# Last query group of an agent-attention and maxout kernel: four of six feature blocks multiplied as pairs of 64-row products in two PSUM banks

## The chip, the cores and the metric

The kernel runs on one core of one Trainium2 chip. The metric is device time in microseconds, the median of several runs. The engines have short names below: PE is TensorE (matrix products; PEld its weight loads), DVE is VectorE, ACT is ScalarE, POOL is GpSimd, and SP is SyncE, which issues the transfers.

## What is computed

Four batches of 12544 query rows with 128 channels attend to 49 agent rows, and the agents attend to all keys. The result goes through a feed-forward layer of width 768 with three input matrices and a maximum over them:

```python
a2k = softmax(agents @ k.T * scale)          # 49 x 12544 a batch
agent_v = a2k @ v                            # 49 x 128
q2a = softmax(q @ agents.T * scale)          # 12544 x 49
x = q2a @ agent_v
h = np.maximum(np.maximum(x @ w1, x @ w2), x @ w3)
out = h @ w_out                              # 50176 x 128, float32
```

## The kernel before

**Tiling.** A batch has 98 tiles of 128 query rows. The kernel works on groups of eight tiles (1024 rows). Groups 0 to 47 hold eight tiles of one batch each; group 48, the last, holds the two tiles that are left of each of the four batches. The agents' values are multiplied into the weights beforehand (tiles G, one a batch), so that a group goes straight from its exponentials to the hidden features. The 768 features are six blocks of 128, numbered f = 0 to 5. The eight tiles of a group are kept as four pairs jj = 0 to 3: the first tile of a pair lies in the upper 64 rows (49 of them used) of the exponentials e.s, the second in the lower 64.

**The operations of a group s**, with the names that the order list uses:
- `u.s.f` and `v.s.f` (PE, `hidden`, L558): the differences w3 - w1 (or w3 - w2 for f = 4) and w2 - w1, for all eight tiles. Each product has 49 rows; products for the upper rows (h = 0) and the lower rows (h = 1) alternate and write different banks. In group 48 each batch has its own G, so that a `u` or `v` is eight products of 128 columns there.
- `a.s.f` (ACT, L571, or L565 for f = 4) takes the positive part of u; `x.s.f` (DVE, L574) takes the maximum with v and writes r.s.f, tile R. For f = 4 v is added onto a in PSUM and ACT writes r.s.4 (L568). r.s.f holds all eight tiles of one feature block, as [128 features, h, 512].
- `li.s.o` (PE, `out_linear`, L582): the part of the output that is linear in x, for half o of the group (pairs 2o and 2o + 1), as two products of 128 rows and 256 columns. It opens the output bank o.s.o.
- `p.s.o.f` (PE, `out_hidden`, L592): four products of 128 rows (the features) and 128 columns that add block f to the half o.
- `su.s`, `re.s`: sums of the exponentials and their reciprocals.
- `ov.s.o` (DVE, `out_scale`, L599): the half o times the reciprocals, into rows 4o to 4o + 3 of the output tile OS.
- `st.s` (SP, L607): the store; in group 48 it is four transfers, each of two rows of OS (one batch).

**What sets the order.** `graph` lists the operations with their costs and needs, but the sequence that runs is the hand-stored list `ORDER` at the end of the file. It is one list for all engines; each engine works off its own operations in that order, and waits are put in where a tile's maker or last reader is on another engine. A number behind a slash names the buffer: `li.48.1/1` opens bank 1 of the class OM, which has two. Bank 1 was that of `o.47.1` and is free when `ov.47.1` has read it; bank 0 was that of `o.47.0`. The `cost` and `mode` given to `add` are notes for a planner and change nothing in the program.

The end of the list before:

```
a.48.4 u.48.3/1 p.47.1.5 x.48.5/11 p.47.1.1 li.48.0/0 a.48.3/0 p.48.0.1 p.48.0.0 v.48.4 ov.47.1 v.48.3/0 x.48.4/7 p.48.0.2
x.48.3/0 st.47 p.48.0.5 li.48.1/1 p.48.1.2 p.48.1.5 p.48.1.4 p.48.0.4 p.48.0.3 p.48.1.3 ov.48.0/2 p.48.1.1 p.48.1.0 ov.48.1 st.48
```

Of the kernel before, what the change touches and what calls it, by code (L numbers as in the profile page):

```python
# [12 lines left out]
ALU = mybir.AluOpType  # L13

P, H, C, A, B, NT, GT, KT, NF = 128, 64, 128, 49, 4, 98, 8, 9, 6
# [4 lines left out]
C31, C21, C1O, WC = 0, DFF, 2 * DFF, 2 * DFF + 2 * C  # L20
CV, CS, CT = KT * A, KT * A + A, (KT - 1) * A
FI = 4
SPARE = 8
FIRST = [KT] * 10 + [4, 4]
LATER = [KT] * 10 + [8]
# [2 lines left out]
PE, ACT, DVE, POOL, SP = range(5)  # L28
ROW, FULL, COL = range(3)
# [11 lines left out]
class Plan:  # L41
# [5 lines left out]
    def add(self, name, eng, fn, cost, mode=FULL, after=(), new=(), use=(), bank=None, serve=0.0):  # L47
        self.index[name] = len(self.ops)
        for cls, t in new:
            self.tiles[t] = cls  # L50
            self.maker[t] = name
        seq = [self.maker[t] for t in use if self.maker[t] not in after]
        self.ops.append(dict(name=name, eng=eng, fn=fn, pace=cost[0], lat=cost[1], mode=mode, after=list(after), seq=seq,
                             new=[t for _, t in new], use=[t for _, t in new] + list(use), bank=bank, serve=serve))
# [21 lines left out]
def parts_of(s):  # L76

    if s < B * WHOLE:
        return [(s // WHOLE, s % WHOLE * GT, GT, 0, GT // 2)]
    return [(b, WHOLE * GT, 2, b, 1) for b in range(B)]  # L80
# [14 lines left out]
def mm(n, cols):  # L95
    t = n * max(cols / 2400 + 0.0025, 0.0253)
    return t, t + 0.235
# [18 lines left out]
def graph(plan, em):  # L116
    add = plan.add
# [4 lines left out]
    for g, (t0, n) in enumerate(ch):  # L122
# [3 lines left out]
            new=[("KB", f"kb0.{g}")], use=[f"k0.{g}"])  # L126
# [4 lines left out]
            new=[("EK", f"e0.{g}")], use=[f"s0.{g}"])  # L131
        add(f"to0.{g}", PE, em.totals(g, n), mm(1, n * 49), after=[f"kx0.{g}"], new=[("OM", "acc")] if g == 0 else [],
            use=[f"e0.{g}"] + (["acc"] if g else []))
        m = n if n == KT else 2
        add(f"vc0.{g}", ACT, em.cast("v", "vb", 0, t0, n, ACT, 0, m), act(m * 128), after=[f"vl0.{g}"], new=[("VB", f"vb0.{g}")],
            use=[f"v0.{g}"])
        if m < n:
            add(f"vd0.{g}", DVE, em.cast("v", "vb", 0, t0, n, DVE, m, n), ((n - m) * 0.067 + 0.08, (n - m) * 0.067 + 0.2),
                after=[f"vl0.{g}"], use=[f"v0.{g}", f"vb0.{g}"])
        add(f"kv0.{g}", PE, em.first_values(g, n), mm(n, 49), after=[f"to0.{g}", f"vc0.{g}"] + ([f"vd0.{g}"] if m < n else []),  # L140
            use=[f"vb0.{g}", f"e0.{g}", "acc"])
# [3 lines left out]
    for w in ("w1", "w3", "w2"):  # L145
# [3 lines left out]
    add("d31a", DVE, em.differences(C31, "w3", "w1", ((0, DFF // 2),)), (0.43, 0.55), after=["lw1a", "lw3a"], use=["w1", "w3"])  # L149
    add("d31b", DVE, em.differences(C31, "w3", "w1", ((DFF // 2, FI * P), (FI * P + P, DFF))), (0.42, 0.54), after=["lw1b", "lw3b"],  # L150
        use=["w1", "w3"])
# [9 lines left out]
        use=["kr0", "acc"])  # L161
    half = DFF // 2
    for name, c, d, eng in (("a", C31, ["d31a"], ACT), ("b", C31 + half, ["d31b", "d32"], DVE), ("c", C21, ["d21a"], ACT),
# [3 lines left out]
            after=[f"gp{name}"], use=[f"gp{name}", "G0"])  # L167
# [7 lines left out]
    for b in range(1, B):  # L175
        ch = chunks(b)
        for g, (t0, n) in enumerate(ch):
            r, m = f"{b}.{g}", f"m.{host_of(b, g)}"
# [10 lines left out]
                use=[m], bank=m)  # L189
            add(f"kv{r}", PE, em.values(b, g, n, m), mm(n, 49), after=[f"kx{r}", f"vc{r}"], use=[m, f"vb{r}", f"e{r}"], bank=m)  # L190
            add(f"va{r}", DVE, em.add_values(b, g, m), (0.13, 0.25), after=[f"kv{r}"] + ([f"va{b}.{g - 1}"] if g else []),
                new=[] if g else [("VA", f"va{b}")], use=[m] + ([f"va{b}"] if g else []), bank=m)
            if g < len(ch) - 1:
                add(f"ea{r}", POOL, em.add_exps(b, g), (0.97, 1.06), after=[f"kx{r}"] + ([f"ea{b}.{g - 1}"] if g else []),
                    new=[] if g else [("EA", f"ea{b}")], use=[f"e{r}"] + ([f"ea{b}"] if g else []))
# [3 lines left out]
            use=[m, f"es{b}", f"e{r}"], bank=m)  # L199
        add(f"nr{b}", DVE, em.normalise(b, m), (0.5, 0.62), after=[f"to{b}", f"va{r}"], new=[("KR", f"kr{b}"), ("G", f"G{b}")],  # L200
            use=[m, f"va{b}"], bank=m)
        for name, c0, c1, eng in (("a", C31, C31 + DFF, ACT), ("c", C21, C21 + DFF, DVE), ("l", C1O, WC, ACT)):
            w = c1 - c0
            add(f"gp{name}{b}", PE, em.product(b, c0, c1, f"gp{name}{b}"), mm(1, w), mode=COL, after=[f"nr{b}", "el"],
                new=[("UV" if w > 512 else "OM", f"gp{name}{b}")])
            add(f"gv{name}{b}", eng, em.product_out(b, c0, c1, c0, f"gp{name}{b}", eng), act(w) if eng == ACT else dve(w),
                after=[f"gp{name}{b}"], use=[f"gp{name}{b}", f"G{b}"])


    for s in range(NQ):  # L210
        parts = parts_of(s)
        gs = [f"G{p[0]}" for p in parts]
        add(f"ql.{s}", SP, em.q_load(s), new=[("LD", f"q.{s}")], **dma(524))
        add(f"qc.{s}", POOL, em.q_cast(s), (1.0, 1.1), after=[f"ql.{s}"], new=[("QB", f"qb.{s}")], use=[f"q.{s}"])
        if s in TURNED:
            add(f"qd.{s}", SP, em.turn_by_dma("qb.", "qT.", s, GT), (1.3, 1.0), after=[f"qc.{s}"], new=[("QT", f"qT.{s}")], use=[f"qb.{s}"],
                serve=0.255 * GT)
        else:
            add(f"qt.{s}", PE, em.q_turn(s), mm(GT, 128), after=[f"qc.{s}", "prep"], new=[("OM", f"qT_ps.{s}")], use=[f"qb.{s}"])
            add(f"qe.{s}", DVE, em.q_evacuate(s), (0.636, 0.735), after=[f"qt.{s}"], new=[("QT", f"qT.{s}")], use=[f"qT_ps.{s}"])  # L220
        add(f"sc.{s}", PE, em.q_scores(s), mm(len(parts), 512 // len(parts)), mode=COL, after=[f"qd.{s}" if s in TURNED else f"qe.{s}"],
            new=[("OM", f"qs.{s}")], use=[f"qT.{s}"])
        add(f"ex.{s}", ACT, em.q_exps(s), (0.56, 0.65), after=[f"sc.{s}"], new=[("EQ", f"e.{s}")], use=[f"qs.{s}"])
        m = f"m.{s}"
        h = s in hosting
        add(f"su.{s}", PE, em.sums(s, m, not h), mm(GT // 2, 2), after=[f"ex.{s}"] + ([f"ks{b}.{g}" for b in range(1, B)
            for g in range(len(LATER)) if host_of(b, g) == s] if h else []), new=[] if h else [("OM", m)], use=[f"e.{s}"] + ([m] if h else []),
            bank=m)
        add(f"re.{s}", DVE, em.recips(s, m), (0.13, 0.25), after=[f"su.{s}"], new=[("RC", f"rc.{s}")], use=[m], bank=m)
        for f in range(NF):  # L230
            def needs(base, first, second):
                out = []
                for p in parts:
                    out.append(f"gv{first if f < 3 else second}" if p[0] == 0 else f"gv{base}{p[0]}")
                return out
            e = f"e.{s}"
            add(f"u.{s}.{f}", PE, em.hidden(s, f, C31, True), mm(len(parts), 512 // len(parts)), mode=ROW,
                after=[f"ex.{s}"] + needs("a", "a", "b"), new=[("UV", f"u.{s}.{f}")], use=[e] + gs)
            if f == FI:
                add(f"a.{s}.{f}", ACT, em.relu_inside(s, f), (0.908, 1.04), after=[f"u.{s}.{f}"], use=[f"u.{s}.{f}"])  # L240
                add(f"v.{s}.{f}", PE, em.hidden(s, f, C21, False), mm(len(parts), 512 // len(parts)), mode=ROW,
                    after=[f"a.{s}.{f}"] + needs("c", "c", "d"), use=[f"u.{s}.{f}", e] + gs)
                add(f"x.{s}.{f}", ACT, em.relu_out(s, f), (0.908, 1.06), after=[f"v.{s}.{f}"], new=[("R", f"r.{s}.{f}")], use=[f"u.{s}.{f}"])
            else:
                add(f"a.{s}.{f}", ACT, em.relu_first(s, f), (0.908, 1.055), after=[f"u.{s}.{f}"], new=[("AS", f"a.{s}.{f}")], use=[f"u.{s}.{f}"])
                add(f"v.{s}.{f}", PE, em.hidden(s, f, C21, True), mm(len(parts), 512 // len(parts)), mode=ROW,
                    after=[f"ex.{s}"] + needs("c", "c", "d"), new=[("UV", f"v.{s}.{f}")], use=[e] + gs)
                add(f"x.{s}.{f}", DVE, em.max_second(s, f), (1.142, 1.26), after=[f"v.{s}.{f}", f"a.{s}.{f}"], new=[("R", f"r.{s}.{f}")],
                    use=[f"v.{s}.{f}", f"a.{s}.{f}"])
        for o in range(2):  # L250
            lin = ["gvl" if p[0] == 0 else f"gvl{p[0]}" for p in parts]
            add(f"li.{s}.{o}", PE, em.out_linear(s, o), mm(2, 256), after=[f"ex.{s}"] + lin, new=[("OM", f"o.{s}.{o}")], use=[f"e.{s}"] + gs)
            for f in range(NF):
                add(f"p.{s}.{o}.{f}", PE, em.out_hidden(s, o, f), mm(4, 128), after=[f"x.{s}.{f}", f"li.{s}.{o}", "cwo"],
                    use=[f"r.{s}.{f}", f"o.{s}.{o}"])
            add(f"ov.{s}.{o}", DVE, em.out_scale(s, o), (0.634, 0.72), after=[f"p.{s}.{o}.{f}" for f in range(NF)] + [f"re.{s}"],
                new=[("OS", f"os.{s}")] if o == 0 else [], use=[f"o.{s}.{o}", f"rc.{s}"] + ([f"os.{s}"] if o else []))
        add(f"st.{s}", SP, em.store(s), after=[f"ov.{s}.0", f"ov.{s}.1"], use=[f"os.{s}"], cost=(0.45, 1.6), serve=524 / 415.0)


class Emit:
# [324 lines left out]
    def out_hidden(self, s, o, f):  # L586
# [6 lines left out]
                                          self.wo_bf[:, f, :], start=False, stop=True, skip_group_check=True)  # L593
        return fn

    def out_scale(self, s, o):
        def fn():
            j = 4 * o
            self.nc.vector.tensor_tensor(out=self.t[f"os.{s}"][:, j:j + 4, :],  # L599
                                         in0=self.t[f"o.{s}.{o}"].rearrange("p (j c) -> p j c", c=C),  # L600
                                         in1=self.t[f"rc.{s}"][:, j:j + 4].unsqueeze(2).to_broadcast([P, 4, C]), op=ALU.mult)
        return fn

    def store(self, s):
# [224 lines left out]
p.46.1.1 v.47.5/1 ov.46.0/2 u.47.3/0 p.46.1.5 a.47.3/1 x.47.5/0 p.46.1.2 p.46.1.4 su.47/0 p.46.1.3 v.47.4 re.47/1 v.47.3/0 ov.46.1  # L829
u.48.1/1 x.47.4/11 li.47.0/0 x.47.3/1 p.47.0.1 st.46 p.47.0.2 a.48.1/2 su.48/1 p.47.0.0 p.47.0.4 re.48/2 v.48.1/2 u.48.5/0  # L830
v.48.0/1 x.48.1/8 a.48.5/1 li.47.1/1 p.47.1.2 p.47.1.0 p.47.1.3 x.48.0/4 p.47.0.3 p.47.1.4 p.47.0.5 u.48.4/2 v.48.5/0 ov.47.0/1
a.48.4 u.48.3/1 p.47.1.5 x.48.5/11 p.47.1.1 li.48.0/0 a.48.3/0 p.48.0.1 p.48.0.0 v.48.4 ov.47.1 v.48.3/0 x.48.4/7 p.48.0.2
x.48.3/0 st.47 p.48.0.5 li.48.1/1 p.48.1.2 p.48.1.5 p.48.1.4 p.48.0.4 p.48.0.3 p.48.1.3 ov.48.0/2 p.48.1.1 p.48.1.0 ov.48.1 st.48
"""


# [28 lines left out]
```

## Time and profile before

| | |
|---|---|
| median of 3 runs | 453.44 us (452.93 to 455.15) |
| span of the profiled execution, first to last instruction | 449.8 us |
| mean granted TensorE clock | 0.996 |
| PE busy | 423.7 us, 94% |
| DVE busy | 402.8 us, 90% |
| ACT busy | 395.1 us, 88% |
| POOL busy | 169.4 us, 38% |
| output products (L592) | 2352, 219 ns each |
| output scalings (L599) | 98, 686 ns each |

The page gives the profiled execution by its span; the median is 3.6 us longer, which lies outside the first and the last instruction. Rows of the timeline read: start in us from the span's start, length in us, engine, line, operation, written tile <- read tiles, count, and in brackets how long the engine was idle before and what ended that. The chain of waits follows the last instruction back to what released it; its rows read start, length, what, count. Matmuls overlap in the pipeline: one takes 0.22 us from start to end while the next starts much sooner, so a busy time of PE is not its rate.

### The profile page before, as it was taken

What the parts mean: (1) busy time and instruction counts of PE and PEld (TensorE: products, weight loads), DVE (VectorE), ACT (ScalarE), POOL (GpSimd) and SP (SyncE); (2) the same over time, 40 slices, a digit from 0 to 9 for tenths busy, and PEclk for the clock granted to TensorE, in tenths of its full rate; (3) what the DMA queues carried; (4) which work ended last, traced back from release to release, by engine and by line L of the source; (5) the groups of instructions that cost most, each with busy time, mean ns of one, the idle gap of its engine ahead of it and who ended that gap; (6) DMA issues with size and microseconds to landing.
All of it is one profiled execution on the core that took longest, in us unless ns stands there. A gap on an engine that the chain in (4) does not pass through costs nothing.

```text
span 449.8 us, 13103 instructions
## 1 busy us (share of the span) xinstructions
PE 423.7 (94%) x5388; PEld 274.0 (61%) x5388; DVE 402.8 (90%) x512; ACT 395.1 (88%) x461; POOL 169.4 (38%) x176
## 2 busy tenths in 40 slices
PE   0778899999999999999999999999999999999996
PEld 0654466666665666666666666666666655565675
DVE  1335999999999999999999999999999999999986
ACT  1459999999988999999989999999889899999983
POOL 1641645455676372464363263453402110100000
PEclk9989999999999999999999999999999999999999
DMA  8999999999999998999969799498608685327142
GB/s 311 409 408 387 326 373 310 263 394 316 340 320 274 392 216 223 408 273 318 406 200 324 216 350 226 141 314 336 212 6 230 191 221 129 96 103 178 48 177 107
DMA packets 80150, 117.80 MB, mean 262 GB/s; under 512 B 53527, under 2 KB 56283, under 8 KB 80091
## 3 DMA queue, kind: packets, MB, share of 16 engines
q1 hardware_dynamic: 79888, 116.87, 83.6%
q8 instruction: 42, 0.69, 0.6%
q14 instruction: 17, 0.14, 0.1%
q10 hardware_dynamic: 203, 0.10, 0.1%
HBM read 78.74 MB, written 25.69 MB: 232 GB/s over the span
## 4 chain that ended last, share of the span: by engine, by line
PE 73%; DMA 12%; DVE 6%; POOL 2%; ACT 2%; SPq 2%; issue 2%; POOLq 0%; DVEq 0%
PE UV L558 29%; PE OM L592 27%; DMA LD<-in_k_dram 6%; PE OM L582 5%; DMA LD<-in_v_dram 4%; DVE R L574 4%; PE OM L523 3%; PE OM L533 3%; PE OM L376 2%; DMA out_dram<-OS 2%; PE OM L359 2%; DVE OS L599 1%; SPq L454 1%; ACT AS L571 1%; ACT VB L333 1%
## 5 line engine op out<-in xcount | busy, mean ns | idle before, releaser
L574 DVE TENSOR_TENSOR R<-UV,AS 128x1024 bf16<-128x1024 f32 x245 | 293.4, 1219 | 11.4 <-PE UV L558 5.3
L571 ACT ACTIVATE AS<-UV 128x1024 bf16<-128x1024 f32 x245 | 246.7, 1023 | 18.3 <-PE UV L558 11.7
L558 PE MATMUL UV<-EQ,G 49*128 49x512 bf16 (+1 forms) x1248 | 178.5, 368 | 2.1 <-DVE R L574 1.3
L592 PE MATMUL OM<-wo_bf,R 128*128 128x128 bf16 x2352 | 179.8, 219 | 0.0
L592 PEld LDWEIGHTS <-R 128*128 128x128 bf16 x2352 | 139.7, 98 | 39.5 <-issue 37.3
L558 PEld LDWEIGHTS <-G 49*128 49x128 bf16 x1248 | 58.7, 93 | 63.9 <-issue 23.8
L517 POOL CAST QB<-LD 128x1024 bf16<-128x1024 f32 x49 | 50.8, 1040 | 111.9 <-DMA LD<-in_q_dram 50.6
L599 DVE TENSOR_TENSOR OS<-OM,RC 128x512 f32<-128x512 f32 x98 | 67.3, 686 | 2.6 <-PE OM L592 1.4
L335 POOL CAST KB<-LD 128x1152 bf16<-128x1152 f32 (+2 forms) x45 | 49.7, 1116 | 40.6 <-DMA LD<-in_k_dram 35.9
L335 POOL CAST VB<-LD 128x1152 bf16<-128x1152 f32 (+1 forms) x33 | 37.3, 1137 | 40.4 <-DMA LD<-in_v_dram 24.3
L568 ACT ACTIVATE R<-UV 128x1024 bf16<-128x1024 f32 x49 | 50.1, 1022 | 2.5 <-PE UV L558 1.7
L565 ACT ACTIVATE UV<-UV 128x1024 f32<-128x1024 f32 x49 | 49.9, 1019 | 2.3 <-DVE R L574 1.2
L582 PE MATMUL OM<-G,EQ 128*128 128x256 bf16 x196 | 37.9, 275 | 0.0
L474 POOL TENSOR_TENSOR EA<-EA,EK 128x441 f32<-128x441 f32 x27 | 27.6, 1023 | 18.5 <-ACT EK L365 18.1
L539 ACT ACTIVATE EQ<-OM 128x512 bf16<-128x512 f32 x49 | 29.4, 601 | 1.0 <-PE OM L533 0.9
L527 DVE COPY QT<-OM 128x1024 bf16<-128x1024 bf16 x38 | 26.0, 684 | 1.1 <-PE OM L523 1.0
L347 DVE COPY KT<-UV 128x1152 bf16<-128x1152 bf16 (+1 forms) x12 | 8.2, 700 | 18.2 <-PE UV L342 18.2
L523 PE MATMUL OM<-ident,QB 128*128 128x128 bf16 x304 | 23.7, 222 | 0.6 <-POOL QB L517 0.6
L582 PEld LDWEIGHTS <-EQ 128*128 128x128 bf16 x196 | 12.3, 97 | 15.9 <-issue 15.2
L523 PEld LDWEIGHTS <-QB 128*128 128x128 bf16 x304 | 18.5, 99 | 4.3 <-issue 2.6
L359 PEld LDWEIGHTS <-KT 128*128 128x128 bf16 x392 | 14.3, 98 | 10.0 <-issue 5.5
L533 PE MATMUL OM<-QT,agT 128*64 128x512 bf16 (+1 forms) x104 | 20.2, 393 | 0.0
(67 smaller groups left out, 196.4 us busy)
## 6 DMA issues: line engine op xcount, KB each, us to landing
LD<-in_q_dram SPq DMA_DIRECT2D x48, 512.0 KB, 6.6
out_dram<-OS SPq DMA_DIRECT2D x48, 512.0 KB, 6.3
LD<-in_k_dram SPq DMA_DIRECT2D x40, 576.0 KB, 7.8
LD<-in_v_dram SPq DMA_DIRECT2D x40, 576.0 KB, 9.4
LD<-in_k_dram SPq DMA_DIRECT2D x3, 512.0 KB, 6.0
LD<-in_v_dram SPq DMA_DIRECT2D x3, 512.0 KB, 11.4
LD<-in_moe_w_dram SPq DMA_DIRECT2D x6, 192.0 KB, 8.4
KT<-KB SPq DMA_TRANSPOSE x33, 6.7
```

The source lines that it names most:

```text
L335: (self.nc.gpsimd if eng == POOL else self.nc.vector).tensor_copy(out=out, in_=src)
L517: return lambda: self.nc.gpsimd.tensor_copy(out=self.t[f"qb.{s}"], in_=self.t[f"q.{s}"][:, :GT, :])
L523: self.nc.tensor.transpose(t[:, j * P:(j + 1) * P], self.t[f"qb.{s}"][:, j, :], self.ident)
L533: self.nc.tensor.matmul(self.t[f"qs.{s}"][h * H:(h + 1) * H, jj * P:(jj + pairs) * P], self.agT[:, b, :], self.t[f"qT.{s}"][:, 2 * jj + h: ...
L558: self.nc.tensor.matmul(t[:, h, jj * P:(jj + pairs) * P], self.t[f"G{b}"][h * H:h * H + A, c + f * P:c + (f + 1) * P], self.t[f"e.{s}"][h ...
L565: return lambda: self.nc.scalar.activation(self.t[f"u.{s}.{f}"], self.t[f"u.{s}.{f}"], AF.Relu)
L568: return lambda: self.nc.scalar.activation(self.t[f"r.{s}.{f}"], self.t[f"u.{s}.{f}"], AF.Relu)
L571: return lambda: self.nc.scalar.activation(self.t[f"a.{s}.{f}"], self.t[f"u.{s}.{f}"], AF.Relu)
L574: return lambda: self.nc.vector.tensor_tensor(out=self.t[f"r.{s}.{f}"], in0=self.t[f"v.{s}.{f}"], in1=self.t[f"a.{s}.{f}"], op=ALU.max)
L582: self.nc.tensor.matmul(self.t[f"o.{s}.{o}"][:, i * 2 * C:(i + 1) * 2 * C], self.t[f"e.{s}"][:, jj * P:(jj + 1) * P], self.t[f"G{of[jj]}"] ...
L592: self.nc.tensor.matmul(self.t[f"o.{s}.{o}"][:, c:c + C], self.t[f"r.{s}.{f}"][:, h, jj * P:(jj + 1) * P], self.wo_bf[:, f, :], start=Fals ...
L599: self.nc.vector.tensor_tensor(out=self.t[f"os.{s}"][:, j:j + 4, :], in0=self.t[f"o.{s}.{o}"].rearrange("p (j c) -> p j c", c=C), in1=self ...
```

## The change

Only group 48 is treated differently (`HALVED = 48`).

- The output banks are cut another way. Before, bank o held the tiles of pairs 2o and 2o + 1. Now bank h holds the first (h = 0) or second (h = 1) tile of each of the four pairs.
- `li.48.h` becomes four products of 49 rows and 128 columns on the upper rows (h = 0) or lower rows (h = 1) of the exponentials.
- For f = 0, 1, 2 and 5, `p.48.x.f` becomes eight products of 64 rows (`out_halves`). They alternate between the upper 64 features and the lower 64. With x = 0 the upper half goes to bank 0 and the lower to bank 1; with x = 1 they change places. Each f still needs both x = 0 and x = 1. For f = 3 and 4 (`WHOLE_F`) the products keep 128 rows (`out_full`).
- `ov.48.0` and `ov.48.1` each need all twelve `p.48`, and write rows 0, 2, 4, 6 and 1, 3, 5, 7 of OS.
- The end of `ORDER` is another: both `li` stand ahead of all `p.48`, and the pairs with x = 1 come last.

```diff
+HALVED, WHOLE_F = 48, (3, 4)
...
+        for f in range(NF):
+            for o in range(2):
+                if s != HALVED:
+                    add(f"p.{s}.{o}.{f}", PE, em.out_hidden(s, o, f), mm(4, 128), after=[f"x.{s}.{f}", f"li.{s}.{o}", "cwo"],
+                        use=[f"r.{s}.{f}", f"o.{s}.{o}"])
+                else:
+                    add(f"p.{s}.{o}.{f}", PE, (em.out_full if f in WHOLE_F else em.out_halves)(s, o, f), mm(4, 128), mode=ROW,
+                        after=[f"x.{s}.{f}", f"li.{s}.0", f"li.{s}.1", "cwo"], use=[f"r.{s}.{f}", f"o.{s}.0", f"o.{s}.1"])
+        for o in range(2):
+            done = [f"p.{s}.{x}.{f}" for f in range(NF) for x in ((0, 1) if s == HALVED else (o,))]
+            add(f"ov.{s}.{o}", DVE, em.out_scale(s, o), (0.634, 0.72), after=done + [f"re.{s}"],
...
+    def out_linear_half(self, s, h):
+        def fn():
+            of = [p[0] for p in parts_of(s) for _ in range(p[4])]
+            r = slice(h * H, h * H + A)
+            for jj in range(GT // 2):
+                self.nc.tensor.matmul(self.t[f"o.{s}.{h}"][:, jj * C:(jj + 1) * C], self.t[f"e.{s}"][r, jj * P:(jj + 1) * P],
+                                      self.t[f"G{of[jj]}"][r, C1O + h * C:C1O + (h + 1) * C], start=(jj == 0), stop=False,
+                                      skip_group_check=True)
+        return fn
+
+    def out_halves(self, s, x, f):
+        def fn():
+            for jj in range(GT // 2):
+                for y in range(2):
+                    h, r = x ^ y, slice(y * H, (y + 1) * H)
+                    self.nc.tensor.matmul(self.t[f"o.{s}.{h}"][:, jj * C:(jj + 1) * C],
+                                          self.t[f"r.{s}.{f}"][r, h, jj * P:(jj + 1) * P], self.wo_bf[r, f, :], start=False, stop=True,
+                                          skip_group_check=True)
+        return fn
+
+    def out_full(self, s, h, f):
+        def fn():
+            for jj in range(GT // 2):
+                self.nc.tensor.matmul(self.t[f"o.{s}.{h}"][:, jj * C:(jj + 1) * C], self.t[f"r.{s}.{f}"][:, h, jj * P:(jj + 1) * P],
+                                      self.wo_bf[:, f, :], start=False, stop=True, skip_group_check=True)
+        return fn
...
     def out_scale(self, s, o):
         def fn():
-            j = 4 * o
-            self.nc.vector.tensor_tensor(out=self.t[f"os.{s}"][:, j:j + 4, :],
+            cut = slice(4 * o, 4 * o + 4) if s != HALVED else slice(o, GT, 2)
+            self.nc.vector.tensor_tensor(out=self.t[f"os.{s}"][:, cut, :],
...
-a.48.4 u.48.3/1 p.47.1.5 x.48.5/11 p.47.1.1 li.48.0/0 a.48.3/0 p.48.0.1 p.48.0.0 v.48.4 ov.47.1 v.48.3/0 x.48.4/7 p.48.0.2
-x.48.3/0 st.47 p.48.0.5 li.48.1/1 p.48.1.2 p.48.1.5 p.48.1.4 p.48.0.4 p.48.0.3 p.48.1.3 ov.48.0/2 p.48.1.1 p.48.1.0 ov.48.1 st.48
+a.48.4 u.48.3/1 p.47.1.5 x.48.5/11 p.47.1.1 a.48.3/0 ov.47.1 st.47 li.48.0/0 li.48.1/1 p.48.0.1 p.48.0.2 p.48.0.0 v.48.4 p.48.0.5 v.48.3/0
+x.48.4/7 x.48.3/0 p.48.1.4 p.48.0.4 p.48.1.3 p.48.0.3 p.48.1.1 p.48.1.2 p.48.1.0 p.48.1.5 ov.48.0/2 ov.48.1 st.48
```

More of the change, by code (lines that the diff above doesn't have):

```diff
@@ L249, in graph @@
                     use=[f"v.{s}.{f}", f"a.{s}.{f}"])
+        lin = ["gvl" if p[0] == 0 else f"gvl{p[0]}" for p in parts]
         for o in range(2):
[L251 to L256, printed above, removed]
+            add(f"li.{s}.{o}", PE, em.out_linear(s, o) if s != HALVED else em.out_linear_half(s, o), mm(2, 256), after=[f"ex.{s}"] + lin,
+                new=[("OM", f"o.{s}.{o}")], use=[f"e.{s}"] + gs)
+        for f in range(NF):
[9 more added lines that the diff above has]
+            add(f"ov.{s}.{o}", DVE, em.out_scale(s, o), (0.634, 0.72), after=done + [f"re.{s}"],
                 new=[("OS", f"os.{s}")] if o == 0 else [], use=[f"o.{s}.{o}", f"rc.{s}"] + ([f"os.{s}"] if o else []))
@@ L594, in out_hidden @@
         return fn
+    def out_linear_half(self, s, h):
[22 more added lines that the diff above has]
+        return fn
     def out_scale(self, s, o):
         def fn():
-            j = 4 * o
-            self.nc.vector.tensor_tensor(out=self.t[f"os.{s}"][:, j:j + 4, :],
+            cut = slice(4 * o, 4 * o + 4) if s != HALVED else slice(o, GT, 2)
+            self.nc.vector.tensor_tensor(out=self.t[f"os.{s}"][:, cut, :],
                                          in0=self.t[f"o.{s}.{o}"].rearrange("p (j c) -> p j c", c=C),
-                                         in1=self.t[f"rc.{s}"][:, j:j + 4].unsqueeze(2).to_broadcast([P, 4, C]), op=ALU.mult)
+                                         in1=self.t[f"rc.{s}"][:, cut].unsqueeze(2).to_broadcast([P, 4, C]), op=ALU.mult)
         return fn
```

## The prediction, made before the changed kernel was run

> **What bounds the kernel now.** I read the page first (busy shares, then the costliest groups), then the chain of waits over the last 25 us, then VectorE's, ScalarE's and SyncE's timelines of the last nine.
>
> ```profile
> span 449.8 us, 13103 instructions
> PE 423.7 (94%) x5388; PEld 274.0 (61%) x5388; DVE 402.8 (90%) x512; ACT 395.1 (88%) x461; POOL 169.4 (38%) x176
> L592 PE MATMUL OM<-wo_bf,R 128*128 128x128 bf16 x2352 | 179.8, 219 | 0.0
> ```
>
> TensorE, VectorE and ScalarE are all near full, so over the span an edit of one engine pays little. The change touches only group 48, the last of 49, so only what ends the span counts. The chain of waits there:
>
> ```profile
> 439.08 1.34 PE OM L592 x24
> 440.42 0.81 PE UV L558 x24
> 441.23 0.55 PE OM L592 x8
> 441.78 0.22 PE OM L582 x2
> 442.00 0.45 PE OM L592 x8
> 442.45 0.55 PE UV L558 x16
> 443.00 0.55 PE OM L592 x8
> 443.55 0.22 PE OM L582 x2
> 443.77 1.13 PE OM L592 x20
> 444.90 0.02 issue
> 444.93 1.36 DVE OS L599 x2
> ```
>
> Columns: start, length, engine, tile, line, count. TensorE works without a hole to 444.90, then VectorE scales the two halves of the output (ov.48.0, ov.48.1) until 446.29. By the order list the rows are: 441.23 p.47.1.5 and p.47.1.1; 441.78 li.48.0; 442.00 p.48.0.1 and p.48.0.0; 442.45 v.48.4 and v.48.3; 443.00 p.48.0.2 and p.48.0.5; 443.55 li.48.1; 443.77 the remaining products, up to p.48.0.3.
>
> The prices stand in these rows. A full product takes 1.34/24 = 0.056 us, and so 8 take 0.45. The 16 products of v.48.4 and v.48.3 are 49-row products in pairs, one in the upper rows, one in the lower, two banks: 0.55 is 8 pairs at 0.056 and 0.10 over. The 8 full products that come after them also take 0.55 and not 0.45. So **a change between full and half-height products costs 0.10**, and **a pair of half-height products takes as long as one full product**.
>
> ```profile
> 440.70 0.68 DVE L599 TENSOR_TENSOR OS<-OM,RC 128x512 f32<-128x512 f32 x1
> 441.29 1.22 DVE L574 TENSOR_TENSOR R<-UV,AS 128x1024 bf16<-128x1024 f32 x1
> 442.42 0.68 DVE L599 TENSOR_TENSOR OS<-OM,RC 128x512 f32<-128x512 f32 x1
> 443.11 1.23 DVE L574 TENSOR_TENSOR R<-UV,AS 128x1024 bf16<-128x1024 f32 x1
> 441.71 1.02 ACT L571 ACTIVATE AS<-UV 128x1024 bf16<-128x1024 f32 x1
> 442.88 1.02 ACT L568 ACTIVATE R<-UV 128x1024 bf16<-128x1024 f32 x1
> 445.65 0.33 SPq L607 DMA_DIRECT2D out_dram<-OS  x1
> 446.55 0.89 SPq L607 DMA_DIRECT2D out_dram<-OS  x2
> 445.65 1.79 SPq L607 DMA_DIRECT2D out_dram<-OS  x4
> ```
>
> VectorE runs ov.47.0, x.48.5, ov.47.1, x.48.3 with no hole; ov.47.1 ends at 442.42 + 0.68 = 443.10. ScalarE runs a.48.3, then x.48.4 at 442.88. SyncE issues the last store as four transfers, one a batch, in 1.79 us. The first goes out at 445.65, when ov.48.0 has ended but ov.48.1 has not, so two of the four are issued under ov.48.1. The last issue ends at 447.44; 2.36 us later the span is over.
>
> **The change, part by part.**
>
> *Amount of TensorE work: nothing.* Features 0, 1, 2 and 5 go from 8 full products each to 16 half ones in 8 pairs: 8 x 0.056 either way. The linear part goes from 4 products of 256 columns (0.22 for two) to 8 of 128. In all 32 + 4 = 36 more products, 5424 on the page. No row shows a 64-row pair. The nearest is the 49-row pair above; a half that waited for its partner would cost 0.056 more. I take 0, with +1.8 as the upper end (32 pairs on the path). Below 0 I see nothing: half-height rows stream 128 columns as full ones do.
>
> *Mode changes.* Those around v.48.4 and v.48.3 go; new ones stand before li.48.0, after v.48.3 and after p.48.0.3. The first two lie in waits (below); the third costs 0.10.
>
> The Trainium skill, "TensorEngine Tiling (Array Packing)", Key Properties, says that a change of tiling mode drains TensorE. The trace agrees, at the 0.10 above: the change saves two of these, 0.2 us, were the rest equal.
>
> *The order: here the time goes.* In the new list li.48.1 stands right behind li.48.0. It writes the bank that ov.47.1 reads, so it waits for 443.10. In the old list six operations stood between, 1.5 us of work that covered that wait. Behind it TensorE now holds p.48.0.1, .2, .0, v.48.4, p.48.0.5 and v.48.3, and for the two v wait ScalarE (x.48.4) and VectorE (x.48.3). ov.47.1 cannot come earlier: VectorE's own order is unchanged. That a waiting matmul holds what is behind it, these rows show:
>
> ```profile
> 137.14 1.21 DVE L574 TENSOR_TENSOR R<-UV,AS 128x1024 bf16<-128x1024 f32 x1
> 138.40 0.39 PE L558 MATMUL UV<-EQ,G 49*128 49x512 bf16 x2 [0.81 <-DVE R L574]
> 138.73 1.07 PE L592 MATMUL OM<-wo_bf,R 128*128 128x128 bf16 x16
> 443.61 0.22 PE L592 MATMUL OM<-wo_bf,R 128*128 128x128 bf16 x1
> ```
>
> TensorE idled 0.81 us for a buffer although 16 products on older tiles stood behind; it started 0.05 after VectorE's end (138.35 to 138.40). The last row: one product takes 0.22 from start to end.
>
> The new last stretch, in starts of products:
> - li.48.0 at 441.78 + 0.10 mode change, done by 442.10, hidden in the wait. li.48.1 at 443.10 + 0.05 = 443.15, four products, to 443.37.
> - p.48.0.1, .2, .0: 12 pairs, 0.67, to 444.04. v.48.4: 4 pairs, the last starts at 444.21 and ends at 444.43. x.48.4 follows 0.10 later (now: v.48.4 ends at 442.78, half way through its row, ScalarE starts at 442.88), so 444.53 + 1.02 = 445.55.
> - p.48.0.5 and v.48.3: to 444.71, the last pair ends at 444.88; x.48.3 from 444.93, + 1.23 = 446.16.
> - p.48.1.4 and p.48.0.4 at 445.55 + 0.05, 8 products, to 446.05. p.48.1.3 and p.48.0.3 at 446.16 + 0.05, 8 products, to 446.66. Mode change 0.10, then p.48.1.1, .2, .0, .5: 16 pairs, 0.90, to 447.66; the last ends at 447.82.
>
> Now the last product ends about 445.57: 12 products (12 x 0.056 = 0.67) after 444.90. So **the waits cost 2.25 us**: the wait at li.48.1 (1.2) and those for x.48.4 and x.48.3 behind it.
>
> *ov.48.0 loses its cover.* Both banks are written to the last pair, so ov.48.0 starts 0.03 after the last product, as it now starts 0.03 after its own (444.90 to 444.93). Now it starts 0.64 before the last product ends: **0.67**. So 447.85, and both scalings end at 449.21. They write every second row of the output tile instead of a contiguous half; no row shows that, I take 0.68 each as now, with 0.1 either side.
>
> *The stores lose theirs.* Each of the four takes two neighbouring rows, one from each scaling, so none can go before ov.48.1 ends. Now the first goes out 0.64 before that end (446.29), then 0.03 after it: **0.67**. First issue 449.24, last ends 449.24 + 1.79 = 451.03. If it could still go early, 0; if issues in a row slow each other, the four together are what I counted.
>
> *Moved at no cost.* st.47 stands earlier in the list, but SyncE's order and its wait for ov.47.1 stay. ScalarE's order stays.
>
> **Sum**: 2.25 + 0.67 + 0.67 = 3.59; the end moves from 447.44 to 451.03, and 2.36 behind it stay. Against the profiled span: 449.8 + 3.6 = 453.4. The median of the three runs is 453.44, that is 3.6 outside the span, which the change does not touch. **Forecast 453.44 + 3.6 = 457.0 us, +0.8%.** Unknowns: pairs 0 to +1.8; li.48.1's products beside the first pairs -0.17, or waiting for weights +0.2; restarts after x.48.4 and x.48.3 up to +0.2; stores -0.67 to 0. That gives 456.2 to 459.2.
>
> **The rivals.**
>
> *A. The pairs do not pair* (9%). Were the 64-row halves to run one after another, 32 pairs cost 0.056 more each: +1.8, **458.8**. For it: no 64-row pair and no two banks swapped in any row. Against it: 24 half-height products in 0.81 with the same layout of rows and banks.
>
> *B. The clock falls in the new waits* (5%).
>
> ```profile
> 27.36:30.77 3.41, 1.63 (x39) 1.33 (x35) 0.76 (x1) 1.59 (x4) 2.34 (x3) 1.00 1.02 407
> 30.77:34.18 3.41, 3.30 (x45) 2.73 (x43) 1.42 (x2) 2.41 (x4) 0.00 (x0) 0.50 1.02 411
> 443.78:447.19 3.41, 1.78 (x32) 1.60 (x29) 1.92 (x3) 0.12 (x1) 0.00 (x0) 1.00 0.56 212
> 447.19:449.80 2.61, 0.00 (x0) 0.00 (x0) 0.00 (x0) 0.00 (x0) 0.00 (x0) 1.00 0.38 125
> ```
>
> Columns: window, length, TensorE busy, four more engines, granted clock. After 3.41 us with TensorE busy for 1.63, the clock stood at 0.50 for 3.41 us; after 3.41 us with 1.78 busy it stayed at 1.00. The new order has at worst 1.7 busy in 3.41 (441.98 to 445.39), just between. If it falls there, 16 products and 16 pairs take 0.11 instead of 0.056, +1.8: **458.8**. It needs the stretch to lie exactly there.
>
> The Trainium skill, "TensorE: Matmul & The Clock Gate", section "Why this matters for your kernels", asks only to avoid idle gaps of over about 3 us, by which this rival could not be. The fall at 30.77 came without one: TensorE was idle for 1.8 of the 3.41 us but still busy for 1.63. I keep the 5%.
>
> *C. The products pass the waiting li.48.1* (10%), the other side. If TensorE ran v.48.4 and v.48.3 while li.48.1 waits, x.48.4 and x.48.3 would come as early as now, TensorE would lose nothing but one mode change, 0.10, and what stays is that and the two lost covers: 0.10 + 0.67 + 0.67 = 1.44, **454.9**, within 0.5% of before. It decides once at least 1.3 of the 2.25 us of waits are won back (3.59 less 0.5%, 2.27). For it: different banks and operands. Against it: the 0.81 us of idle above.
>
> **How the numbers follow.** Forecast 76%, A 9%, B 5%, C 10%. Half a per cent, about what a measurement of this kernel can tell from no change, is 2.27 us: 455.71. The runs of before spread from 452.93 to 455.15, so I put 3% of the forecast below that line, and 1% of C above it. Slower 73 + 14 + 1 = 88% and within the bound 3 + 9 = 12%; I take 1% from each for what no case names and give it to faster: 87%, 11%, 2%. Range: the bounds 456.2 to 459.2, down by the 0.5 that the lowest run lies below the median: 455.7 to 459.2. It leaves out C and little else.
>
> **What the new profile would show.** Waits: TensorE idle for about 1.2 us ahead of li.48.1, put down to VectorE's ov.47.1; again 0.7 to 0.9 before p.48.1.4 and 0.15 before p.48.1.3. Order of ends: last product at about 447.8, ov.48.0 right behind it, four stores in one row from about 449.2. Pairs: 16 half products in about 0.45. Wrong if TensorE has no hole between 442 and 443, if the first store is issued ahead of ov.48.1's end, or if the half products are 0.056 apart each; if VectorE's ov.47.1 ends at another time than 443.1, all times after it move along.

## The result and the profile after

The changed kernel takes 456.0 us (median of 18 runs, 454.53 to 457.6), the kernel before, in runs beside it, 452.71 (18 runs). The ratio is 1.0073, with a 95% interval of 1.0056 to 1.0089, so **3.3 us slower, between 2.5 and 4.0**. Forecast were 3.6 us, and 457.0 in all over a base of 453.44 that came from three runs. The profiled execution has a span of 452.8 us and took 454.99 in all: 2.2 us lie outside the span. Every execution on record with both figures has 1.8 to 2.5 there, so the 3.6 us read from the table of before set a median against a span of another execution. The forecast only adds to the median, so this changes nothing in it. Runs of one kernel spread over 3 to 4 us, and much of that arises ahead of the change: the order list of all kernels here is the same but for its last two lines, and VectorE's own order is the same down to ov.47.1, yet that scaling ends at 443.11 us in the profile of before, at 442.51 in that of the changed kernel, and between 441.81 and 444.57 in those of the experiments. Below, the end of the program is therefore measured from the end of ov.47.1. The last product repeats to 0.01 us between kernels that share an order (2.45 and 2.46; 4.79 four times, in the table below), and the span ends 2.34 to 2.36 us behind the last issue in all seven kernels that issue four stores in a row on SyncE.

The chain of waits of the changed kernel, its last 13 us (start, length, what):

```profile
439.83 0.82 PE UV L567 x24
440.65 0.05 issue
440.70 1.21 DVE R L583
441.91 0.61 DVE OS L635
442.52 0.04 issue
442.56 0.21 PE OM L610
...
443.94 1.03 ACT R L577
444.97 0.05 issue
445.02 0.62 PE OM L628 x8
445.64 0.04 issue
445.68 0.62 PE OM L628 x8
446.30 1.02 PE OM L620 x32
447.32 0.02 issue
447.34 0.69 DVE OS L635
```

Before, this stretch was TensorE alone down to the output scalings. Now it changes engine five times: VectorE for x.48.5 and ov.47.1 (440.70, 441.91), TensorE from li.48.1 to v.48.4, ScalarE for x.48.4 (443.94), TensorE again for the full products (L628) and the sixteen pairs with x = 1 (446.30), then VectorE. While the chain is away from TensorE, TensorE stands still for much of the time. The timelines of the changed kernel say how long and for whom (in brackets: idle before, and what ended it). The single row behind them is VectorE's in the kernel before:

```profile
441.83 0.68 DVE L635 TENSOR_TENSOR OS<-OM,RC 128x512 f32<-128x512 f32 x1
442.56 0.21 PE L610 MATMUL OM<-G,EQ 49*128 49x128 bf16 x1 [1.05 <-DVE OS L635]
442.58 0.23 PE L620 MATMUL OM<-wo_bf,R 64*128 64x128 bf16 x1
442.62 0.21 PE L610 MATMUL OM<-G,EQ 49*128 49x128 bf16 x1
443.88 0.41 PE L567 MATMUL UV<-EQ,G 49*128 49x128 bf16 x5
444.40 1.22 DVE L583 TENSOR_TENSOR R<-UV,AS 128x1024 bf16<-128x1024 f32 x1 [1.89 <-PE UV L567]
445.02 1.28 PE L628 MATMUL OM<-wo_bf,R 128*128 128x128 bf16 x16 [0.72 <-ACT R L577]
446.23 1.07 PE L620 MATMUL OM<-wo_bf,R 64*128 64x128 bf16 x32
447.34 1.29 DVE L635 TENSOR_TENSOR OS<-OM,RC 128x512 f32<-128x512 f32 x2 [1.72 <-PE OM L620]
448.66 1.80 SPq L643 DMA_DIRECT2D out_dram<-OS  x4
```

```profile
444.93 1.36 DVE L599 TENSOR_TENSOR OS<-OM,RC 128x512 f32<-128x512 f32 x2 [0.59 <-PE OM L592]
```

TensorE idles 1.05 us until ov.47.1 has read the bank of li.48.1, then 0.72 until x.48.4 is done. VectorE, which before went straight from ov.47.1 to x.48.3 and idled 0.59 ahead of ov.48.0, idles 1.89 and 1.72. The sixteen pairs of 64-row products (x32) take 1.07 us from the first start to the last end. Less the 0.22 of the last product itself that is 0.85 for a little over fifteen steps: about 0.056 a pair, as a full product. And all four stores go out in one row, after both scalings.

### The profile page after: what moved, and what is told of

It reads as the page before. It is cut to its first block, busy times and chain, and to the rows that moved or that the text cites. A ratio compares the mean times of both kernels' runs of the same rounds, so it can differ in the third digit from the quotient of the medians.

```text
span 452.8 us, 13175 instructions
## 1 busy us (share of the span) xinstructions
PE 423.2 (93%) x5424; PEld 273.0 (60%) x5424; DVE 403.4 (89%) x512; ACT 395.3 (87%) x461; POOL 169.3 (37%) x176
## 4 chain that ended last, share of the span: by engine, by line
PE 72%; DMA 13%; DVE 6%; SPq 2%; issue 2%; POOL 2%; ACT 2%; DVEq 0%; POOLq 0%; ACTq 0%
PE UV L567 28%; PE OM L601 26%; DMA LD<-in_v_dram 9%; PE OM L591 5%; DVE R L583 4%; PE OM L532 3%; PE OM L542 3%; DMA LD<-in_k_dram 2%; PE OM L385 2%; DMA out_dram<-OS 2%; PE OM L368 2%; SPq L334 1%; DVE OS L635 1%; SPq L463 1%; ACT AS L580 1%
## 5 line engine op out<-in xcount | busy, mean ns | idle before, releaser
L601 PE MATMUL OM<-wo_bf,R 128*128 128x128 bf16 x2304 | 176.6, 220 | 0.0
L601 PEld LDWEIGHTS <-R 128*128 128x128 bf16 x2304 | 136.9, 98 | 39.5 <-issue 37.5
```

The source lines that it names most:

```text
L601: self.nc.tensor.matmul(self.t[f"o.{s}.{o}"][:, c:c + C], self.t[f"r.{s}.{f}"][:, h, jj * P:(jj + 1) * P], self.wo_bf[:, f, :], start=Fals ...
```

## The experiments

The theory on trial was the one of the prediction: the wait at li.48.1 and what is queued behind it, then the two lost covers. The main rival was that the 64-row products or their two banks cost the time. Times are from the end of ov.47.1, each from one profiled execution:

| kernel | last product ends | last scaling ends | last store issued | span ends | ratio to before (95%) |
|---|---|---|---|---|---|
| before | 2.45 | 3.18 | 4.33 | 6.68 | 1 |
| changed | 4.79 | 6.12 | 7.95 | 10.30 | 1.0073 (1.0056 to 1.0089) |
| e1_order_alone | 5.00 | 5.73 | 6.66 | 9.00 | 1.0051 (1.0033 to 1.0068) |
| e7_li_late | 3.46 | 4.19 | 5.12 | 7.47 | 1.0024 (1.0001 to 1.0046) |
| e2_v_first | 3.33 | 4.66 | 6.48 | 8.84 | 1.0042 (1.0019 to 1.0064) |
| e3_pairs_fill | 3.87 | 5.20 | 7.01 | 9.37 | 1.0023 (1.0000 to 1.0046) |
| e8_quarters | 4.79 | 6.25 | 7.41 | 9.76 | 1.0061 (1.0039 to 1.0084) |
| e5_two_queues | 4.79 | 6.12 | 7.01 | 10.04 | 1.0063 (1.0042 to 1.0084) |
| e4_one_store | 4.79 | 6.12 | 6.53 | 10.20 | 1.0087 (1.0056 to 1.0118) |
| e6_before_two_queues | 2.46 | 3.19 | 3.58 | 6.43 | 0.9990 (0.9969 to 1.0012) |

### e1_order_alone: the new order without the 64-row products

```diff
-(the end of ORDER in the kernel before)
+a.48.4 u.48.3/1 p.47.1.5 x.48.5/11 p.47.1.1 a.48.3/0 ov.47.1 st.47 li.48.0/0 li.48.1/1 p.48.0.1 p.48.0.2 p.48.0.0 v.48.4 p.48.0.5 v.48.3/0
+x.48.4/7 x.48.3/0 p.48.1.4 p.48.0.4 p.48.1.3 p.48.0.3 p.48.1.1 p.48.1.2 p.48.1.0 p.48.1.5 ov.48.0/2 ov.48.1 st.48
```

> The kernel before (full products, banks by halves of the group) with the list's end in the changed kernel's order: both li ahead of all p.48, v.48.4 and v.48.3 behind them. Theory (the order makes the waits): TensorE waits 1.0 to 1.2 us ahead of li.48.1 and 0.7 ahead of p.48.1.4; the last product ends 4.9 us after ov.47.1 ends (before: 2.45), the last store issue ends 6.6 after it (before: 4.33), and the median is 2.3 us above before. ov.48.0 and two stores keep their cover. Rival (the 64-row products and their two banks cost the time, the order nothing): last product 2.5 us after ov.47.1, median within 0.3 us of before.

Its timelines, with ov.47.1 first (443.89 + 0.68 = 444.57):

```profile
443.89 0.68 DVE L599 TENSOR_TENSOR OS<-OM,RC 128x512 f32<-128x512 f32 x1
444.62 0.38 PE L582 MATMUL OM<-G,EQ 128*128 128x256 bf16 x2 [1.16 <-DVE OS L599]
447.19 0.62 PE L592 MATMUL OM<-wo_bf,R 128*128 128x128 bf16 x8 [0.52 <-ACT R L568]
448.06 1.51 PE L592 MATMUL OM<-wo_bf,R 128*128 128x128 bf16 x24 [0.25 <-DVE R L574]
448.72 0.69 DVE L599 TENSOR_TENSOR OS<-OM,RC 128x512 f32<-128x512 f32 x1 [0.71 <-PE OM L592]
449.61 0.69 DVE L599 TENSOR_TENSOR OS<-OM,RC 128x512 f32<-128x512 f32 x1 [0.20 <-PE OM L592]
```

There is no 64-row product in this kernel, and the three waits are there: 1.16 for ov.47.1, 0.52 for x.48.4, 0.25 for x.48.3. The last product comes 2.55 us later than before and the span ends 2.32 later (expected 2.3). The two scalings stand apart here: ov.48.0 runs while the last sixteen products do, so its cover is kept, and with it the early stores. The rival as it stands, that the order costs nothing, falls; what the two banks cost is read from e2_v_first.

In one and the same order the changed kernel's last product comes 0.21 us earlier than this one's (4.79 against 5.00). Full products change mode around each of the two v. The 64-row products need two changes fewer outside the waits, at 0.10 each. That is what they are worth by themselves in this order.

### e7_li_late: only li.48.1 moved back

```diff
-... li.48.0/0 li.48.1/1 p.48.0.1 p.48.0.2 p.48.0.0 v.48.4 p.48.0.5 v.48.3/0
+... li.48.0/0 p.48.0.1 p.48.0.2 p.48.0.0 v.48.4 p.48.0.5 v.48.3/0 li.48.1/1
```

> As e1_order_alone (full products), but li.48.1 alone moved back, behind v.48.3. Theory (li.48.1's place makes the first wait): no wait ahead of li.48.1, last product 3.5 us after ov.47.1 (e1: 4.9), last store issue 5.2 after it, median 0.8 above before; what stays is that v.48.4 and v.48.3 stand behind 12 products. Rival (the place of the v products alone makes the waits, li.48.1 none): as e1, 2.3 above before.

```profile
443.48 0.68 DVE L599 TENSOR_TENSOR OS<-OM,RC 128x512 f32<-128x512 f32 x1
444.64 0.39 PE L582 MATMUL OM<-G,EQ 128*128 128x256 bf16 x2
445.23 0.62 PE L592 MATMUL OM<-wo_bf,R 128*128 128x128 bf16 x8 [0.20 <-ACT R L568]
446.10 1.51 PE L592 MATMUL OM<-wo_bf,R 128*128 128x128 bf16 x24 [0.25 <-DVE R L574]
```

Against e1_order_alone one operation has moved. li.48.1 (L582) has no bracket any more: it starts at 444.64, 0.48 after ov.47.1 has ended, because TensorE was busy until then. The last product ends at 3.46 instead of 5.00, so **the place of li.48.1 alone is worth 1.5 us**. What is left of the waits, 0.20 and 0.25, comes from v.48.4 standing behind twelve other products and v.48.3 behind sixteen.

### e2_v_first: the 64-row products with the v products ahead of li.48.1

```diff
-... li.48.0/0 li.48.1/1 p.48.0.1 p.48.0.2 p.48.0.0 v.48.4 p.48.0.5 v.48.3/0
-x.48.4/7 x.48.3/0 p.48.1.4 p.48.0.4 p.48.1.3 p.48.0.3 p.48.1.1 ...
+... li.48.0/0 v.48.4 v.48.3/0 x.48.4/7 x.48.3/0 li.48.1/1 p.48.0.1 p.48.0.2
+p.48.0.0 p.48.0.5 fe.48 p.48.0.4 p.48.0.3 p.48.1.4 p.48.1.3 p.48.1.1 ...
+    def fence(self, s):
+        return lambda: self.nc.vector.tensor_copy(out=self.scrap, in_=self.t[f"o.{s}.1"][:, 4 * C - 1:4 * C])
```

> The changed kernel with v.48.4 and v.48.3 ahead of li.48.1, and the full products right behind the first pairs; one VectorE copy of one column is added between the pairs of x = 0 and those of x = 1, because v.48.3 and x.48.3 no longer stand between them. Theory (the waits come from what is queued behind li.48.1): x.48.4 and x.48.3 come as early as before, the last product ends 3.3 us after ov.47.1 (changed kernel: 4.79), the last store issue 6.5 after it (changed: 7.95), the median is 1.5 us below the changed kernel and 2.1 above before, the two lost covers staying. Rival (the 64-row products cost the time): like the changed kernel, last product 4.8 us after ov.47.1, median 3.3 above before.

```profile
441.92 0.68 DVE L641 TENSOR_TENSOR OS<-OM,RC 128x512 f32<-128x512 f32 x1
442.12 1.03 ACT L580 ACTIVATE R<-UV 128x1024 bf16<-128x1024 f32 x1
442.57 1.22 DVE L586 TENSOR_TENSOR R<-UV,AS 128x1024 bf16<-128x1024 f32 x1
442.66 0.21 PE L613 MATMUL OM<-G,EQ 49*128 49x128 bf16 x1 [0.20 <-DVE OS L641]
443.87 1.07 PE L634 MATMUL OM<-wo_bf,R 128*128 128x128 bf16 x16
443.97 0.16 DVE L629 COPY scrap<-OM 128x1 f32<-128x1 f32 x1 [0.18 <-PE OM L623]
444.87 1.07 PE L623 MATMUL OM<-wo_bf,R 64*128 64x128 bf16 x32
445.98 1.29 DVE L641 TENSOR_TENSOR OS<-OM,RC 128x512 f32<-128x512 f32 x2 [1.84 <-PE OM L623]
```

x.48.3 runs at 442.57, right behind ov.47.1, and x.48.4 at 442.12: as early as before the change. The full products and the last pairs follow without a bracket. The 64-row products are all still there, and the last product ends at 3.33 instead of 4.79. The span ends 1.46 earlier than the changed kernel's, and 2.16 later than before, where 2.1 was expected.

So another order wins back 1.46 us, and 2.16 stay, with the way the banks are cut. Of these, 1.28 are the two lost covers. The other 0.88 stand ahead of the last product (3.33 against 2.45). Every pair writes both banks, so none can start before ov.47.1 has freed bank 1; here all output products of group 48 follow li.48.1 at 442.66. Before, eleven of the 48 had started when ov.47.1 ended. An estimate from the prices of the prediction: eleven at 0.056, two mode changes at 0.10 and a restart of 0.05 make 0.87.

The added copy takes over what v.48.3 and x.48.3 do at their place in the changed order. Pairs with x = 0 and pairs with x = 1 write the same bank from different halves of the rows, and both kernels keep them apart. In the changed kernel that is TensorE's wait for x.48.3, whose input was made behind the last pair with x = 0. The Trainium skill, "TensorEngine Tiling (Array Packing)", Gotcha 1, says that different row tiles cannot access one PSUM bank at the same time and that the program must keep them apart; no run here tried the two kinds without a separation.

### e3_pairs_fill: the pairs with x = 1 moved into the waits

```diff
-... p.48.0.0 v.48.4 p.48.0.5 v.48.3/0 x.48.4/7 x.48.3/0 p.48.1.4 p.48.0.4 p.48.1.3 p.48.0.3 p.48.1.1 p.48.1.2 p.48.1.0 p.48.1.5 ...
+... p.48.0.0 v.48.4 p.48.0.5 fe.48 v.48.3/0 x.48.4/7 x.48.3/0 p.48.1.1 p.48.1.2 p.48.1.0 p.48.1.5 p.48.1.4 p.48.0.4 p.48.1.3 p.48.0.3 ...
```

> The changed kernel with the sixteen pairs of x = 1 ahead of the full products of features 4 and 3, and one VectorE copy of one column between the two kinds of pairs. Theory (TensorE waits for x.48.4 and x.48.3 because nothing ready stands ahead of p.48.1.4): the pairs fill these two waits, the wait ahead of li.48.1 (1.0) stays, the last product ends 3.9 us after ov.47.1 (changed kernel 4.79), the span ends 9.4 after it (10.30). Rival (the pairs in the second order of banks run slower than 0.056 a pair): last product later than 4.3.

```profile
444.27 1.02 ACT L580 ACTIVATE R<-UV 128x1024 bf16<-128x1024 f32 x1 [1.80 <-PE UV L570]
444.64 1.07 PE L623 MATMUL OM<-wo_bf,R 64*128 64x128 bf16 x32
444.73 1.23 DVE L586 TENSOR_TENSOR R<-UV,AS 128x1024 bf16<-128x1024 f32 x1
445.65 1.07 PE L634 MATMUL OM<-wo_bf,R 128*128 128x128 bf16 x16
```

The 32 products now run beside x.48.4 and x.48.3, and the last product ends at 3.87 (expected 3.9): the waits for x.48.4 and x.48.3 cost 0.9 us because nothing that was ready stood ahead of p.48.1.4. The ratio agrees: its interval ends at 1.0046, below that of the changed kernel, which begins at 1.0056.

### e4_one_store, e5_two_queues, e8_quarters: where the stores' 0.67 us lie

```diff
# e4: one transfer
+            if s == B * WHOLE:
+                out = self.io["out"].rearrange("(b t) c -> b t c", b=B)[:, WHOLE * GT * P:, :]
+                for b0, b1 in ((0, 4),):
+                    self.nc.sync.dma_start(out[b0:b1].rearrange("b (p j) c -> p b (j c)", j=2), ...)
# e5: every second transfer from ScalarE
+                q = self.nc.scalar if s == B * WHOLE and i % 2 else self.nc.sync
# e8: four scalings of 256 columns, by batches
+                for h in range(2):
+                    cut = slice(4 * o + h, 4 * o + 4, 2)
```

> The changed kernel with the last group's store as one transfer of four batches instead of four transfers. Theory (the stores' cost is the issue of four in a row on SyncE, 1.79 us): last product as in the changed kernel (4.8 us after ov.47.1), the store issue ends 0.5 us after ov.48.1 instead of 1.83, and the span and the median are 1.3 us shorter than the changed kernel, 2.0 above before. Rival (the end is set by the bytes landing, not by the issues): the last landing comes as late as with four transfers, median as the changed kernel, 3.3 above before.

In e4_one_store the single issue on SyncE, and the last group's transfers of e4_one_store and of the changed kernel (count, size of each, median us from issue to landing):

```profile
447.96 0.38 SPq L645 DMA_DIRECT2D out_dram<-OS  x1
out_dram<-OS SPq DMA_DIRECT2D x1, 512.0 KB, 2.9
out_dram<-OS SPq DMA_DIRECT2D x4, 128.0 KB, 1.8
```

It ends at 448.34, 0.4 after the last scaling, where the changed kernel's last of four ended 1.83 after it. But the span goes on for 3.66 us behind it, to 452.0; in the changed kernel 2.34 us are left behind the last issue (450.46 to 452.8). 1.42 us of issue are saved and 1.32 of them given back: the span ends at 10.20 instead of 10.30. **The theory of this run is refuted**: without the row of issues the end comes only 0.10 earlier and not 1.3, because the one large transfer takes 2.9 us to land and a small one 1.8.

> The changed kernel with the second and fourth of the last group's four transfers issued by ScalarE instead of SyncE. Theory as it stands after e4_one_store (the end follows from 512 KB that must land after ov.48.1; one transfer landed 2.9 us after its issue began): issues end 0.9 us earlier, but the span ends as in the changed kernel, 10.2 to 10.3 us after ov.47.1. Rival (four issues in a row on SyncE set it): the span ends 0.8 us earlier, 9.5 after ov.47.1.

The two queues of e5_two_queues:

```profile
449.75 0.81 SPq L644 DMA_DIRECT2D out_dram<-OS  x2
449.76 0.86 ACTq L644 DMA_DIRECT2D out_dram<-OS  x2
out_dram<-OS SPq DMA_DIRECT2D x2, 128.0 KB, 2.0
out_dram<-OS ACTq DMA_DIRECT2D x2, 128.0 KB, 2.3
```

The four issues end 0.94 us earlier, the span 0.26: between the theory (no gain) and the rival (0.8), nearer the theory. Issued faster, the transfers take longer to land, 2.0 and 2.3 us where they took 1.8. So two limits lie close together here. With four issues in a row the end follows the last issue by 2.35 us; with the issues out of the way, the landing of the 512 KB allows 0.1 to 0.3 us less.

> The changed kernel with each scaling cut in two by batches: the first two tiles' pairs of both banks first, then the others, four scalings of 256 columns, so that the first two transfers can go before the last scalings. Theory (the last group loses because no transfer goes before the last scaling ends): scalings take 0.25 to 0.4 us longer in all, two transfers go early, the span ends 0.4 to 0.6 us earlier than the changed kernel, 9.7 to 9.9 us after ov.47.1. Rival (the early transfers are worth nothing): 10.5 to 10.7, later by the longer scalings.

In e8_quarters the scalings and the issues:

```profile
448.43 1.41 DVE L637 TENSOR_TENSOR OS<-OM,RC 128x256 f32<-128x256 f32 x4 [1.72 <-PE OM L620]
449.21 1.79 SPq L650 DMA_DIRECT2D out_dram<-OS  x4
```

The first transfer is issued at 449.21, while the last two scalings still run (to 449.84). The four scalings take 1.41 us instead of 1.29 (0.12 longer, where at least 0.25 was expected), and the span ends 0.54 us earlier all the same, as expected. Counted from the last scaling, the last issue ends 1.16 later, as before the change (1.15), and not 1.83: two transfers ahead of the last scaling are worth the 0.67 that the prediction gave for them. The ratios of these three cannot be told from the changed kernel's.

### e6_before_two_queues: the same in the kernel before

> The kernel before with the second and fourth of the last group's four transfers issued by ScalarE. If the issues in a row set the end: the last issue ends 0.65 us earlier and so does the span, 6.0 us after ov.47.1 (before: 6.68), median 0.7 below before. If the landing of the bytes sets it: 6.4 to 6.7, no difference that can be measured.

The edit is that of e5_two_queues, in the kernel before. The issues end 0.75 earlier, the span at 6.43 instead of 6.68: 0.25, as in e5_two_queues. In the whole that is no difference that can be measured (0.9990, 0.9969 to 1.0012). No version here beats the kernel before.

## Why the prediction was right

Its sum was 3.59 us; from ov.47.1 to the last store issue the trace shows 7.95 - 4.33 = 3.62, to the end of the span 10.30 - 6.68 = 3.62. Its three terms, 2.25 + 0.67 + 0.67, measured 2.34 + 0.60 + 0.68; two small errors cancel. The runs give 3.3 (2.5 to 4.0).

- **The wait at li.48.1.** TensorE was to restart 0.05 after ov.47.1: it did (0.05). It idled 1.05 us ahead, where about 1.2 was named. e1 and e7 show that this place alone makes the wait.
- **x.48.4 and x.48.3 behind it.** Measured from ov.47.1, x.48.4 was to start at 1.43 and to end at 2.45; it did. x.48.3 was to start at 1.83 and started at 1.89: I had taken 0.05 from the last product to VectorE, it was 0.11.
- **Last product.** Forecast at 4.72 (447.82 - 443.10), measured 4.79, of which 0.06 are x.48.3's. That is 4.79 - 2.45 = 2.34 instead of 2.25. The prediction puts all of it down to the order; e2 shows that 0.88 of it stays in a better order, since the banks keep every output product behind ov.47.1.
- **ov.48.0's cover.** It starts 0.04 after the last product, as forecast with 0.03; the two scalings took 1.29 and not 1.36, which gave 0.07 back. Rows written with a gap between them cost nothing that shows.
- **The stores.** First issue 0.03 after ov.48.1, four in 1.80, as forecast. The step holds in size and in mechanism: e8 gives two transfers their head start back and wins the 0.67. What the prediction did not have is the second limit, the landing, which shows as soon as the issues go faster (e4, e5).
- **The price of the products** held: sixteen pairs at 0.056. So did the mode change ahead of them: they start at 446.23, and the eight products from 445.68 (8 x 0.056 = 0.45) would have let them start 0.10 earlier. But the sentence that the change saves two mode changes is wrong by the prediction's own list: two go and three come, of which two lie in waits.

Rival A (no pairing) falls by that row, rival C by the 1.05 us of idle time and by e1 and e7. Rival B, the clock:

```profile
441.61:445.02 3.41, 1.73 (x53) 1.56 (x52) 1.52 (x3) 1.55 (x2) 0.00 (x0) 1.00 0.39 149
445.02:447.30 2.28, 2.24 (x48) 1.79 (x48) 0.60 (x1) 0.00 (x0) 0.00 (x0) 1.00 0.05 14
32.92:36.33 3.41, 2.16 (x47) 1.51 (x46) 0.63 (x2) 3.23 (x5) 0.00 (x0) 1.00 1.02 403
36.33:39.75 3.42, 3.40 (x40) 2.10 (x38) 1.96 (x4) 3.10 (x6) 0.00 (x0) 0.50 1.05 387
```

These windows of the changed kernel have TensorE's busy time after the length and the granted clock third from the end. Where the two waits lie closest TensorE was busy for 1.73 of 3.41 us, as forecast (1.7), and the clock stayed at 1.00. It fell only behind the last product (mean 0.69 from 448.63 to 450.46), where no product is left to slow. But the share of busy time, by which the prediction judged this rival, does not decide it: earlier in the same trace the clock fell to 0.50 after 3.41 us with 2.16 busy (32.92 to 36.33). That it held through the waits is therefore measured and not explained, and as far as the runs show it is luck that the forecast came out right on this point. The Trainium skill, "TensorE: Matmul & The Clock Gate", section "Why this matters for your kernels", asks to avoid idle gaps of over about 3 us. The waits here (1.05 and 0.72) are shorter and the clock held, but ahead of the fall at 36.33 no gap was longer than 0.61 us either, so the trace does not follow that bound.

What the 64-row products gain is the 0.21 us that the comparison with e1_order_alone shows, little beside the 3.62 us that the whole costs. In no order tried here does the change come out ahead.

## What to carry to other kernels

A product that waited for its bank held everything queued behind it on TensorE, so ask of each moved operation what stood between it and its buffer's release, and who waits for what now stands behind it. Splitting work so that two results finish together takes away the cover of whatever followed the first one: here one scaling and half of the last store. Work that writes two buffers at once also cannot start before the later of the two is free. And where runs spread more than the effect, count from an event that the change does not touch; here that read single steps to 0.1 us and less.

## What the runs showed of the hardware

- Half-height products of two different operations share the array when they lie in different halves of the rows: li.48.1 (49 rows, lower half, 442.56, 442.62) runs interleaved with products of p.48.0.1 (442.58), which by the order in the code are those of the upper half, in the changed kernel's rows above. I had put a possible 0.17 on that. It gave nothing that shows: x.48.4 started when forecast without it. The lower half seems to fall behind by the four products of li.48.1: the stretch ends with five products of v.48.3 (443.88), 0.05 apart, of which four are left without a partner.
- One transfer of 512 KB landed 2.9 us after its issue began, four of 128 KB in a row 1.8 us each (median), so fewer issues were worth 0.1 us. Four of 128 KB from two engines landed after 2.0 and 2.3 us, and two issuing engines were worth 0.26 us.
